# Output tiles of four tokens by 32 positions, and twelve of 28 weight pairs split into two words at each use

## The chip, the cores and the metric

One core of a Trainium2 chip runs the whole program. The metric is the device time of one execution in microseconds. Three runs of the kernel before gave 1483.95, 1479.09 and 1470.52 us, median 1479.09. TensorE multiplies (PE, its weight loads PEld), VectorE (DVE) and ScalarE (ACT) do elementwise work, GpSimd (POOL) and SyncE (SP) issue the DMAs.

## What is computed

Inputs are eight sequences of 576 positions; everything is in 32-bit floats.

```python
p_packed = attention(p, k, v)             # 32 packed queries a head, 8 heads of 64
x = attention(q, p_packed, p_packed)      # [8, 576, 512]
# mixer: xk, xr mix each position with the one before it
kk = relu(xk @ w_k) ** 2                  # 512 -> 1024
x = sigmoid(xr @ w_r) * (kk @ w_v)
# last block
u = x + (x.T @ U @ V).T                   # mixes positions, rank 32
out = u + relu(u @ w_ch1) @ w_ch2         # 512 -> 2048 -> 512
```

The first two parts take about the first half of the time, the last block the second.

## The kernel before

Each 32-bit operand of a matmul is split into a high part that a matmul takes exactly and a low rest ("hi" by a copy to the type fp32r, "lo" by a subtraction), and each product is three matmuls: hi by hi, hi by lo, lo by hi (`PASS`). The last block's two layers are each done with seven block products instead of eight (sums of blocks are formed first). Its weights are combined once, while the mixer runs (`make_ws`, `make_t`), split, and put in DRAM: 56 first-layer products lie in 28 pairs `ws_d0` to `ws_d27`, 512 KB each, and the second layer's in `t_d`.

The 36 token tiles of 128 tokens are worked on in six **steps** (s = 0 to 5) of six tiles. A step is a **window A** (`window_a`: first layer, 8 blocks f of 7 products, 336 matmuls named psc) and a **window B** (`window_b`: second layer, seven stages of 48 matmuls named psX, psY, psZ, psW). Weights come from DRAM again in every step, a pair at a time, through a ring of six tiles (`load_w`, pool `ring`, issued from POOL's queue; a load waits until PE is done with the pair six before). In A, ACT takes products out of PSUM (`p`, `hid`) and DVE sums them into `hid`; in B, ACT and DVE split `hid` into `sp` (three tiles) for PE.

Next to that, the step after is prepared. In A: SP loads its rows of x (`load_u`, tiles `u`, from `x2_d`, which the trace calls x_d) and, where a new pair of sequences begins, `xa` from `xu_d` (`load_xu`); DVE and ACT make `X` of xa (`sum_xu`); PE forms psh from X and the stretched V (`vst`); DVE adds it to u (`h_block`), turns it (`t_block`, 32 by 32 blocks), SP stores the turned tile to `uq_d` and loads it back in another order into `y` (`Turned.fill`). In B, ACT and DVE make the next step's operands `ob` from y (`operand_steps`). The results are added into y and turned back (`o`), and SP stores them (`send`).

A tile was 64 positions by two tokens i (`halves_of`: 576 positions of a sequence are 64 rows by 9 tokens; the ninth token has a tile of its own for both sequences). So a u load was two DMAs of 64 rows, and a tile's output eight stores of 32 KB: four by 128 columns, two by token.

The order on every engine is made before the run by the class `Plan`: each operation has predecessors, priority class and an assumed cost, and `emit` walks through time and gives every engine the operation it finds ready first; DVE and ACT take the earliest ready, PE and SP the earliest written. On the chip each engine takes its instructions strictly in this order, and so does each DMA queue's issuing engine.

Of the kernel before, what the change touches and what calls it, by code (L numbers as in the profile page):

```python
# [9 lines left out]
F32 = mybir.dt.float32  # L10
# [486 lines left out]
def packed_attention_moe_mixer_kernel(  # L497
# [707 lines left out]
    vst_ = []  # L1205

    def make_v():
        vst = plan.tile(vx_p, [P, 12, 64], F32R, "vst")
        vst_.append(vst)
        plan.zero(vst[:, NI:NI + 2].bitcast(F32))  # L1210
        for c in range(2):
            raw = plan.tile(st_p, [P, 512], F32, "s", parts=(0, 1, 2, 3), name="raw_v")
            for g in range(4):
                plan.dma(raw.at(g)[g * 32:(g + 1) * 32, 0:288], v_d[:, c * 288:(c + 1) * 288])
            rv = raw[:, 0:288].rearrange("p (c i) -> p i c", i=NI)
            to = vst[:, 0:NI, c * 32:(c + 1) * 32]
            plan.copy(to, rv, ("dve",))
            for g in (1, 3):
                gr = slice(g * 32, (g + 1) * 32)
                plan.tt(to[gr], rv[gr], to[gr], sub)  # L1220
        plan.copy(vst[:, NI + 2], vst[:, NI - 1], ("dve",))
# [33 lines left out]
    def make_ws(f):  # L1255
        a11, a12, a21, a22 = [t[:, h * 256:(h + 1) * 256] for t in raw_pair(w1_d, f) for h in range(2)]
        s1, s2, s3, s4 = four_sums()
        plan.tt(s1, a21, a22, add)
        plan.tt(s2, s1, a11, sub)
        plan.tt(s3, a11, a21, sub)  # L1260
        plan.tt(s4, a12, s2, sub)
        for i, src in enumerate((a11, s2, s1, a12, s3, s4, a22)):
            n, h = divmod(ws_at[f, i], 2)
            put_split(bl_ws, src, ws_d[n].at(h)[:, h * 512:(h + 1) * 512])

    def make_t(f):
# [12 lines left out]
        plan.tt(t3, b12, b22, sub)  # L1279
        plan.tt(t4, b21, t2, sub)  # L1280
        g, h = divmod(f, 2)
        for i, src in enumerate((b11, b21, b22, t4, t1, t2, t3)):
            put_split(bl_ws, src, t_d[i][g].at(h)[:, h * 512:(h + 1) * 512], by_block)

    def load_w(src):
        t = plan.tile(ring_p, [P, 2, 2, 256], F32R, "ring")
# [17 lines left out]
            plan.tt(X[64:128, :], xa[64:128], X[64:128, :], sub)  # L1304
            xt[b, b2] = X

    def halves_of(T):
        b, t = divmod(T, NI)
        if t == NI - 1:
            return b, [(slice(0, P), t, slice(0, P))]  # L1310
        b2, k2 = divmod(t, 4)
        return b, [(slice(e * 64, (e + 1) * 64), 2 * k2 + e, slice(b2 * 64, (b2 + 1) * 64)) for e in range(2)]

    def slot(n, name):
        if n < 4:
# [1 line left out]
        return plan.tile(st_p, [P, DM], F32, "s", parts=(0, 1), name=name)  # L1317

    def u_of(T):
        return ug[T][0]  # L1320

    def load_u(T, after=()):
        b, hs = halves_of(T)
        if T >= 6:
            u = slot(T % 6, "u")
            ug[T] = u, u.at(0), u.at(1)
        else:
            t = T % 2
            if t == 0:
                first_u[T] = plan.tile(cv.st, [P, 2, DM], F32, "st", parts=(0, 1, 2, 3), name="u")  # L1330
            u = first_u[T - t][:, t]
            ug[T] = u.on((2 * t, 2 * t + 1)), u.on(2 * t), u.on(2 * t + 1)
# [9 lines left out]
    def h_block(T, after=()):  # L1342
        b, t = divmod(T, NI)
        ps = plan.bank(prep_banks[0], "psh", prep_banks[0] is ps_a,
                       [plan.wr[x] for x in u_of(T).keys()] + list(after))
        if t < NI - 1:
            k2 = t % 4
            plan.mm(ps, vst_[0][:, 2 * k2:2 * k2 + 2].rearrange("p e c -> p (e c)"), xt[b, t // 4],
                    start=True, stop=True)
        else:  # L1350
            for b2 in range(2):
                plan.mm(ps, vst_[0][:, NI - 1 + 2 * b2:NI + 1 + 2 * b2].rearrange("p e c -> p (e c)"), xt[b, b2],
                        start=(b2 == 0), stop=(b2 == 1))
        u = u_of(T)
        if T >= 6:
            plan.tt(u, ps, u, add)
            return
        to = slot(T, "u") if T < 4 else first_u[0].on((2 * T - 8, 2 * T - 7))[:, T - 4]
        plan.tt(by_channel(to, "j m"), by_channel(ps, "m j"), by_channel(u, "m j"), add)
        ug[T] = (to,)  # L1360

    class Turned:

# [71 lines left out]
    def operand_steps(s):  # L1435
# [8 lines left out]
        for i, src in enumerate((b11, t2, t1, b21, t1, b22, t2)):  # L1444
# [27 lines left out]
    def product(s, f, i, ps, fresh):  # L1472
        n, e = divmod(ws_at[f, i], 2)
        if e == 0:
            wpair[0] = load_w(ws_d[n])
        w, x = wpair[0][:, e], ops[s][i]
        out = ps[:, 0:CW]
        c = 0
        for k in range(2):
            for wi, a in PASS:  # L1480
                plan.mm(out, w[:, wi, k * P:(k + 1) * P],
                        half(x, a)[:, k * CW:(k + 1) * CW],
                        start=(fresh and c == 0), stop=(c == 5), skip_group_check=True)
                c += 1
# [251 lines left out]
    for s in range(NS):  # L1736
        prep = {f: [] for f in range(NF)}
        more = iter(())
        if s + 1 < NS:
# [3 lines left out]
            for n in range(6):  # L1743
# [50 lines left out]
```

## Time and profile before

| | |
|---|---|
| runs, median (lowest to highest) | 1479.09 us (1470.52 to 1483.95) |
| the profiled execution | 1474.71 us, span 1472.9 us |
| PE busy / DVE / ACT / POOL | 95% / 75% / 48% / 18% of the span |
| mean granted TensorE clock | 0.972 |
| moved by DMA | 349.5 MB, 237 GB/s over the span |
| steps 0 to 5 begin at | 701, 829, 951, 1093, 1218, 1342 us; the last matmul ends near 1458 us |

The profile is of one execution. Times are from the start of its span. In rows of groups, "L259 DVE TENSOR_TENSOR sp<-hid,sp" is an instruction of VectorE that line 259 of the kernel (a helper) issued, writing a tile named sp and reading hid and sp. An idle time is put down to what ended it.

### The profile page before, as it was taken

How to read it: one execution, taken by the hardware profiler on the slowest of the kernel's cores; microseconds unless marked ns; L12 is line 12 of the kernel's file. 1: busy time of each engine (PE TensorE's matmuls, PEld its weight loads, DVE VectorE, ACT ScalarE, POOL GpSimd, SP SyncE). 2: the span in 40 equal slices, each digit the busy share in tenths (PEclk: the TensorE clock that was granted, in tenths of full speed). 3: DMA queues.
4: the chain of work that ended last, by engine and by line, in shares of the span. 5: the costliest groups of instructions: out<-in, count | busy, mean ns of one | idle time of the engine just before them, and what ended most of it. 6: DMA issues, size and time to landing. Idle time of an engine off the chain costs nothing.

```text
span 1472.9 us, 24029 instructions
## 1 busy us (share of the span) xinstructions
PE 1400.9 (95%) x8464; PEld 1277.0 (87%) x8464; DVE 1100.1 (75%) x2125; ACT 701.2 (48%) x1395; POOL 265.6 (18%) x502
## 2 busy tenths in 40 slices
PE   7889999999999999999998999979898999999996
PEld 5557888888888888888998998969798999999995
DVE  6777968778888989888577767836675795696475
ACT  5657656666666767676224223312332342242231
POOL 0000011321111111000222222212122222222220
PEclk8789999999999999999999999989999999999998
DMA  8853347767665768788998999999899989999985
GB/s 233 249 167 137 114 108 169 194 147 182 158 174 166 250 242 279 270 308 280 272 301 230 286 305 302 258 281 248 235 267 302 316 251 298 307 266 289 264 251 136
DMA packets 224584, 349.50 MB, mean 237 GB/s; under 512 B 92912, under 2 KB 138800, under 8 KB 224464
## 3 DMA queue, kind: packets, MB, share of 16 engines
q0 software_dynamic: 59264, 210.94, 48.4%
q1 hardware_dynamic: 165200, 137.02, 34.2%
q8 instruction: 67, 1.10, 0.3%
q14 instruction: 53, 0.43, 0.1%
HBM read 273.35 MB, written 74.52 MB: 236 GB/s over the span
## 4 chain that ended last, share of the span: by engine, by line
PE 65%; issue 14%; DMA 9%; POOL 4%; ACT 3%; DVE 3%; SPq 2%; POOLq 0%; DVEq 0%; ACTq 0%
PE psv L197 12%; PE psk L197 12%; PE psc L197 10%; PE psX L197 7%; PE psr L197 7%; PE psZ L197 4%; PE psat L197 4%; POOL ring L324 4%; PE psat L213 2%; PE psY L197 2%; PE psW L197 2%; DMA u<-x_d 2%; SPq L324 2%; DMA kin<-in_k_dram 1%; DMA ring<-t_d 1%
## 5 line engine op out<-in xcount | busy, mean ns | idle before, releaser
L197 PE MATMUL psc<-ob,ring 128*128 128x384 f32 x2016 | 358.8, 337 | 1.8 <-DVE hid L259 1.7
L197 PEld LDWEIGHTS psc<-ob,ring 128*128 128x128 f32 x2016 | 354.2, 190 | 5.1 <-DVE hid L259 2.7
L197 PE MATMUL psv<-w,kk 128*128 128x512 f32 x783 | 200.9, 395 | 0.0
L197 PE MATMUL psX<-sp,ring 128*128 128x384 f32 x864 | 161.5, 343 | 16.2 <-ACT sp L293 11.2
L259 DVE TENSOR_TENSOR hid<-p,psc 128x384 f32<-128x384 f32 x144 | 78.8, 549 | 130.4 <-PE psc L197 130.3
L293 ACT ACTIVATE p<-psc 128x384 f32<-128x384 f32 x96 | 47.3, 492 | 263.4 <-PE psc L197 255.8
L197 PEld LDWEIGHTS psX<-sp,ring 128*128 128x128 f32 x864 | 153.9, 193 | 21.3 <-ACT sp L293 12.5
L197 PEld LDWEIGHTS psv<-w,kk 128*128 128x128 f32 x783 | 144.5, 188 | 29.1 <-issue 2.3
L293 ACT ACTIVATE sp<-hid 128x768 fp32r<-128x768 f32 x120 | 100.7, 845 | 120.3 <-PE psX L197 56.2
L259 DVE TENSOR_TENSOR sp<-hid,sp 128x768 fp32r<-128x768 f32 x120 | 113.5, 952 | 48.4 <-ACT sp L293 47.6
L324 POOL DMA_DIRECT2D ring<-ws_d x168 | 90.4, 538 | 313.2 <-PE psc L197 233.7
L324 POOL DMA_DIRECT2D ring<-t_d x168 | 90.3, 538 | 286.5 <-PE psX L197 130.3
L197 PE MATMUL psk<-xk,w 128*128 128x384 f32 x528 | 104.4, 340 | 0.3 <-DVE w L278 0.3
L197 PE MATMUL psZ<-sp,ring 128*128 128x384 f32 x576 | 101.8, 334 | 0.0
L197 PEld LDWEIGHTS psZ<-sp,ring 128*128 128x128 f32 x576 | 100.0, 188 | 0.0
L197 PEld LDWEIGHTS psk<-xk,w 128*128 128x128 f32 x528 | 92.8, 188 | 5.4 <-DVE w L278 0.8
L197 PE MATMUL psr<-wA,xr 128*128 128x512 f32 x315 | 86.8, 403 | 0.0
L238 ACT ACTIVATE sq<-psk 128x384 f32<-128x384 f32 x96 | 46.4, 489 | 72.2 <-PE psk L197 71.6
L278 DVE SCALAR_TENSOR_TENSOR hid<-hid 128x384 f32<-128x384 f32 (+1 forms) x96 | 72.3, 753 | 3.1
L197 PEld LDWEIGHTS psr<-wA,xr 128*128 128x128 f32 x315 | 58.9, 192 | 13.1 <-issue 0.9
L324 POOL DMA_DIRECT2D st<-in_moe_w_ch_dram x80 | 44.0, 554 | 136.1 <-DVE m L278 128.9
L238 ACT ACTIVATE sp<-hid 128x768 fp32r<-128x768 f32 x48 | 40.7, 848 | 56.3 <-PE psX L197 41.0
(199 smaller groups left out, 2364.2 us busy)
## 6 DMA issues: line engine op xcount, KB each, us to landing
ring<-ws_d POOLq DMA_DIRECT2D x168, 512.0 KB, 5.1
ring<-t_d POOLq DMA_DIRECT2D x168, 512.0 KB, 4.8
ws_d<-bl SPq DMA_DIRECT2D x56, 256.0 KB, 4.1
t_d<-bl SPq DMA_DIRECT2D x56, 256.0 KB, 3.9
x_d<-xo SPq DMA_DIRECT2D x16, 576.0 KB, 3.3
x_d<-x POOLq DMA_DIRECT2D x36, 256.0 KB, 2.8
kin<-in_k_dram SPq DMA_DIRECT2D x32, 256.0 KB, 5.6
vin<-in_v_dram SPq DMA_DIRECT2D x32, 256.0 KB, 3.6
```

The source lines that it names most:

```text
L197: self.nc.tensor.matmul(o, l, r, start=start, stop=stop, **k)
L213: self.nc.tensor.transpose(out.get(), in_.get(), ident.get())
L238: self.nc.scalar.activation(o, in_.get(), func, **k)
L259: return self.elem(engs, lambda e, o, x, y: e.tensor_tensor(out=o, in0=x, in1=y, op=op), out, [a, b], self.TT, cls)
L278: ("dve",), lambda e, o, x, y: e.scalar_tensor_tensor(out=o, in0=x, scalar=s, in1=y, op0=op0, op1=op1), out, [a, b], self.TT, cls)
L293: self.nc.scalar.activation(o, i, AF.Copy)
L324: (self.nc.sync if eng == "sp" else self.nc.gpsimd).dma_start(out=o, in_=i)
```

## The change

Three things change. First, a tile is now 32 positions by four tokens (`rows_of`). A u load is one DMA, a tile's output four stores of 64 KB (24 stores in every step), and `vst` is laid out so that four tokens by 32 columns stand together. Second, of the 28 pairs the twelve with odd numbers from 5 to 27 (`RAW`) stay as plain 32-bit words in DRAM, 256 KB each. `make_ws` writes the block sums there without splitting them, and in every step `load_words` loads the words into one of four buffers, ACT copies hi into a ring tile and DVE subtracts for lo. Two of the buffers are spare parts of the operand tiles (`spare`), two lie in a tile that the mixer used (`words`). Third, t_block is listed for block 4 + n // 3 in place of 4 + n // 2.

```diff
+    RAW = tuple(range(5, 28, 2))
-    ws_d = [dtile(f"ws_d{n}", [P, 1024], (0, 1)) for n in range(7 * NF // 2)]
+    ws_d = [dtile(f"ws_d{n}", [P, (1024, 512)[n in RAW]], (0, 1)) for n in range(7 * NF // 2)]
...
             n, h = divmod(ws_at[f, i], 2)
-            put_split(bl_ws, src, ws_d[n].at(h)[:, h * 512:(h + 1) * 512])
+            if n in RAW:
+                plan.dma(ws_d[n].at(h)[:, h * 256:(h + 1) * 256], src)
+            else:
+                put_split(bl_ws, src, ws_d[n].at(h)[:, h * 512:(h + 1) * 512])
...
+    words = {}
+
+    def load_words(s, src):
+        if not words:
+            t = plan.tile(ust_p, [P, NI * P], F32, "ust", parts=(0, 1), name="words")
+            words.update((i, t.at(i)[:, i * 512:(i + 1) * 512]) for i in range(2))
+        i = words["n"] = words.get("n", -1) + 1
+        raw = words[i % 2] if i % 4 > 1 else spare[s, i % 2]
+        plan.dma(raw, src, eng="pool", slack=2000.0)
+        t = plan.tile(ring_p, [P, 2, 2, 256], F32R, "ring", parts=(0, 1))
+        hi, lo = [t.at(a)[:, :, a] for a in range(2)]
+        raw = raw.rearrange("p (e c) -> p e c", e=2)
+        plan.copy(hi, raw, ("act",))
+        plan.tt(lo, raw, hi, sub)
+        return t
...
-    def halves_of(T):
+    def rows_of(T):
         b, t = divmod(T, NI)
         if t == NI - 1:
-            return b, [(slice(0, P), t, slice(0, P))]
-        b2, k2 = divmod(t, 4)
-        return b, [(slice(e * 64, (e + 1) * 64), 2 * k2 + e, slice(b2 * 64, (b2 + 1) * 64)) for e in range(2)]
+            return b, slice(0, P), slice(t, NI)
+        w, i = divmod(t, 2)
+        return b, slice(w * 32, (w + 1) * 32), slice(4 * i, 4 * i + 4)
...
-        for n, (to, i, rows) in enumerate(hs):
-            dst = ug[T][1 + n] if len(hs) > 1 else ug[T][0]
-            plan.dma(dst[to], x2_d[b].at(i)[rows, i * DM:(i + 1) * DM], after=after)
+        src = x2_d[b].on(tuple(range(i.start, i.stop)))[rows, i.start * DM:i.stop * DM]
+        plan.dma(ug[T], src.rearrange("p (a c) -> a p c", c=DM) if i.stop - i.start > 1 else src, after=after)
...
-            wpair[0] = load_w(ws_d[n])
-        w, x = wpair[0][:, e], ops[s][i]
+            wpair[0] = load_words(s, ws_d[n]) if n in RAW else load_w(ws_d[n])
+        w = [wpair[0].on(a if n in RAW else 0)[:, e, a] for a in range(2)]
+        x = ops[s][i]
...
-                for to, i, rows in hs:
-                    plan.dma(dst[rows, i, m * P:(m + 1) * P].rearrange("(a p) c -> p a c", p=32),
-                             src[:, to.start // 32:to.stop // 32])
+                to = dst[:, :, m * P:(m + 1) * P]
+                if i.stop == NI:
+                    to = to.rearrange("(a p) i c -> p (a i) c", p=32)
+                plan.dma(to, src)
...
-                prep[4 + n // 2].append(lambda o, T=T: t_block(T))
+                prep[4 + n // 3].append(lambda o, T=T: t_block(T))
```

What moves shows in the orders. On SP, from the end of step 1 into window A of step 2 (x_d is `x2_d`, out_dram the output), there stood:

```order
L324 DMA y<-uq_d_234 32x4x384 x4
L324 DMA out_dram<-o 32x2x128 x40
L324 DMA out_dram<-o 32x4x128 x4
L324 DMA u<-x_d_71 64x512 x8
L324 DMA xa<-xu_d_75 32x512 x8
L324 DMA uq_d_235<-turned 128x1536
```

and now stands:

```order
L324 DMA y<-uq_d_234 32x4x384 x4
L324 DMA out_dram<-o 32x4x128 x24
L324 DMA u<-x_d_71 128x1x512 x4
L324 DMA xa<-xu_d_75 32x512 x8
L324 DMA uq_d_235<-turned 128x1536
```

Ahead of the xa loads SP has 24 stores and 4 loads in place of 44 and 8.

On ACT, at the end of window A and the first stages of window B of step 2 (p and hid are window A's last, the three ob copies make the next step's operands from y, sums are built from y too), there stood:

```order
L293 ACTIVATE p_11162<-psc_11223 128x384
L293 ACTIVATE ob<-y 128x4x6x32
L238 ACTIVATE hid<-psc_11201 128x384
L293 ACTIVATE ob<-y 128x4x6x32
L293 ACTIVATE sp<-hid 128x768
L238 ACTIVATE sp<-hid 128x768 x4
L293 ACTIVATE ob<-y 128x4x6x32
L293 ACTIVATE sp<-hid 128x768 x6
L293 ACTIVATE ob<-sums 128x4x6x32
```

and now stands:

```order
L293 ACTIVATE p_11135<-psc_11117 128x384
L238 ACTIVATE hid<-psc_11114 128x384
L293 ACTIVATE ob<-y 128x4x6x32 x2
L293 ACTIVATE sp<-hid 128x768
L238 ACTIVATE sp<-hid 128x768 x4
L293 ACTIVATE sp<-hid 128x768 x2
L293 ACTIVATE ob<-y 128x4x6x32
L293 ACTIVATE sp<-hid 128x768 x2
L293 ACTIVATE ob<-sums 128x4x6x32
```

The third ob copy stands behind seven sp copies in place of five; in step 0 it is seven in place of six.

On DVE, in the middle of window A of step 2, where X is made for the next step (u, turned: the next step's tiles; hid: this step's sums), there stood:

```order
L278 SCALAR_TENSOR_TENSOR hid<-hid 128x384
L296 CAST X_9986<-xa 128x512
L259 TENSOR_TENSOR hid<-p_10759,psc_10941 128x384
L259 TENSOR_TENSOR X_9981<-xa,X_9981 64x512
L259 TENSOR_TENSOR X_9986<-xa,X_9986 64x512
L259 TENSOR_TENSOR hid<-p_10854,psc_10993 128x384
L259 TENSOR_TENSOR u<-psh,u 128x512 x2
L220 STREAM_TRANSPOSE turned<-u 128x16x32 x2
L259 TENSOR_TENSOR hid<-p_10854,psc_10993 128x384
```

and now stands:

```order
L259 TENSOR_TENSOR ring<-words,ring 128x2x256
L278 SCALAR_TENSOR_TENSOR hid<-hid 128x384
L259 TENSOR_TENSOR hid<-p_10723,psc_10860 128x384
L259 TENSOR_TENSOR X_9932<-xa,X_9932 64x512
L259 TENSOR_TENSOR hid<-p_10801,psc_10920 128x384
L259 TENSOR_TENSOR X_9935<-xa,X_9935 64x512
L259 TENSOR_TENSOR u<-psh,u 128x512 x2
L220 STREAM_TRANSPOSE turned<-u 128x16x32
L259 TENSOR_TENSOR ring<-ob,ring 128x2x256
L259 TENSOR_TENSOR hid<-p_10801,psc_10920 128x384
L220 STREAM_TRANSPOSE turned<-u 128x16x32
```

The subtractions for lo (ring<-words, ring<-ob) stand between the hid sums, X at the same place among them; both casts of X are ACT's now.

## Rows read from the trace of the kernel before

**Rows 1.** Stages: us, busy PE PEld DVE ACT POOL (instructions), clock, DMA share, GB/s.

```profile
340.00:700.00 360.00, 359.11 (x2075) 308.33 (x2075) 315.32 (x713) 243.83 (x535) 48.09 (x91) 1.00 0.72 230
...
700.60:761.40 60.80, 60.80 (x350) 59.92 (x349) 36.37 (x66) 16.10 (x30) 16.15 (x30) 1.00 0.98 274
761.40:829.20 67.80, 61.66 (x338) 60.01 (x338) 52.48 (x68) 25.48 (x31) 15.06 (x28) 0.95 0.93 260
...
951.40:1026.00 74.60, 63.01 (x348) 62.33 (x348) 38.84 (x71) 16.33 (x30) 15.05 (x28) 0.91 0.98 263
1026.00:1093.40 67.40, 60.85 (x333) 59.84 (x333) 50.96 (x66) 24.73 (x30) 15.05 (x28) 0.95 0.91 244
1093.40:1160.20 66.80, 62.57 (x345) 61.57 (x344) 38.53 (x70) 16.45 (x30) 15.05 (x28) 0.95 1.08 304
1341.60:1399.80 58.20, 58.20 (x337) 58.20 (x336) 29.75 (x55) 14.36 (x27) 15.06 (x28) 1.00 0.97 287
1399.80:1458.20 58.40, 58.40 (x337) 58.09 (x336) 44.36 (x63) 21.21 (x25) 12.36 (x23) 1.00 0.80 228
```

**Rows 2.** PE's waits from 700 us on: total us, times, longest.

```profile
PE psh L197 <- DVE X L259: 15.7, 2, 11.6
PE psX L197 <- ACT sp L293: 11.2, 4, 5.7
PE psX L197 <- DMA ring<-t_d: 2.6, 4, 1.2
```

**Rows 3.** Waits of the whole run, same columns.

```profile
DVE hid L259 <- PE psc L197: 131.7, 113, 3.5
...
ACT ob L293 <- DMA y<-uq_d: 31.5, 9, 9.4
...
DVE X L296 <- DMA xa<-xu_d: 16.5, 2, 11.6
```

**Rows 4.** Timeline of SP's issues, 930 to 1010: start, us taken, count.

```profile
948.60 25.50 SPq L324 DMA_DIRECT2D out_dram<-o  x44
974.14 5.38 SPq L324 DMA_DIRECT2D u<-x_d  x8
979.57 9.28 SPq L324 DMA_DIRECT2D xa<-xu_d  x8
```

**Rows 5.** Timeline of PE in B0 and in B2; idle time before in brackets.

```profile
786.95 0.69 PE L197 MATMUL psX<-sp,ring 128*128 128x384 f32 x1 [4.64 <-ACT sp L293]
...
1048.59 0.69 PE L197 MATMUL psX<-sp,ring 128*128 128x384 f32 x1 [5.71 <-ACT sp L293]
```

**Rows 6.** DMA, 1024 to 1047: POOL's q0, SP's q1 (packets, MB); issues.

```profile
q0 software_dynamic: 1737, 6.33, 89.8%
q1 hardware_dynamic: 1467, 1.29, 41.7%
...
y<-uq_d SPq DMA_DIRECT2D x8, 96.0 KB, 14.1
```

**Rows 7.** DMA issues, 951 to 1012: count, KB, median us to landing.

```profile
y<-uq_d SPq DMA_DIRECT2D x3, 96.0 KB, 5.1
out_dram<-o SPq DMA_DIRECT2D x4, 64.0 KB, 4.8
```

**Rows 8.** Groups by line and form, 690 to 1473: busy us, mean ns.

```profile
L259 DVE TENSOR_TENSOR X<-xa,X 64x512 fp32r<-64x512 f32 x6 | 3.9, 688 | 0.1
L293 ACT ACTIVATE X<-xa 128x512 fp32r<-128x512 f32 x3 | 1.9, 631 | 12.2 <-DMA xa<-xu_d 12.0
```

**Rows 9.** SP's last stores: four of 64 KB, then 24 of 32 KB.

```profile
1455.94 1.83 SPq L324 DMA_DIRECT2D out_dram<-o  x4
...
1459.31 11.12 SPq L324 DMA_DIRECT2D out_dram<-o  x24
```

**Rows 10.** DMA issues, 1440 to 1473: columns as in rows 7.

```profile
out_dram<-o SPq DMA_DIRECT2D x40, 32.0 KB, 1.6
out_dram<-o SPq DMA_DIRECT2D x4, 64.0 KB, 1.8
```

More of the change, by code (lines that the diff above doesn't have):

```diff
@@ L1207, in make_v @@
     def make_v():
-        vst = plan.tile(vx_p, [P, 12, 64], F32R, "vst")
+        vst = plan.tile(vx_p, [P, 768], F32R, "vst")
         vst_.append(vst)
-        plan.zero(vst[:, NI:NI + 2].bitcast(F32))
+        plan.zero(vst[:, 576:704].bitcast(F32))
         for c in range(2):
@@ L1215, in make_v @@
             rv = raw[:, 0:288].rearrange("p (c i) -> p i c", i=NI)
[L1216 to L1221, printed above, removed]
+            for to, i0, i1 in ((vst[:, c * 256:(c + 1) * 256], 0, 8), (vst[:, 512 + c * 32:544 + c * 32], 8, NI)):
+                to = to.rearrange("p (i c) -> p i c", c=32)
+                plan.copy(to, rv[:, i0:i1], ("dve",))
+                for g in (1, 3):
+                    gr = slice(g * 32, (g + 1) * 32)
+                    plan.tt(to[gr], rv[gr, i0:i1], to[gr], sub)
+        plan.copy(vst[:, 704:768], vst[:, 512:576], ("dve",))
     def raw_pair(src, f):
@@ L1283, in make_t @@
             put_split(bl_ws, src, t_d[i][g].at(h)[:, h * 512:(h + 1) * 512], by_block)
+    words = {}
[12 more added lines that the diff above has]
+        return t
+    spare = {}
     def load_w(src):
@@ L1319, in u_of @@
     def u_of(T):
-        return ug[T][0]
+        return ug[T]
     def load_u(T, after=()):
-        b, hs = halves_of(T)
+        b, rows, i = rows_of(T)
         if T >= 6:
-            u = slot(T % 6, "u")
-            ug[T] = u, u.at(0), u.at(1)
+            ug[T] = slot(T % 6, "u")
         else:
@@ L1329, in load_u @@
             if t == 0:
-                first_u[T] = plan.tile(cv.st, [P, 2, DM], F32, "st", parts=(0, 1, 2, 3), name="u")
-            u = first_u[T - t][:, t]
-            ug[T] = u.on((2 * t, 2 * t + 1)), u.on(2 * t), u.on(2 * t + 1)
-        for n, (to, i, rows) in enumerate(hs):
-            dst = ug[T][1 + n] if len(hs) > 1 else ug[T][0]
-            plan.dma(dst[to], x2_d[b].at(i)[rows, i * DM:(i + 1) * DM], after=after)
+                first_u[T] = plan.tile(cv.st, [P, 2, DM], F32, "st", parts=(0, 1), name="u")
+            ug[T] = first_u[T - t].on(t)[:, t]
+        src = x2_d[b].on(tuple(range(i.start, i.stop)))[rows, i.start * DM:i.stop * DM]
+        plan.dma(ug[T], src.rearrange("p (a c) -> a p c", c=DM) if i.stop - i.start > 1 else src, after=after)
     prep_banks = [ps_a]
@@ L1346, in h_block @@
         if t < NI - 1:
-            k2 = t % 4
-            plan.mm(ps, vst_[0][:, 2 * k2:2 * k2 + 2].rearrange("p e c -> p (e c)"), xt[b, t // 4],
+            plan.mm(ps, vst_[0][:, t % 4 * P:(t % 4 + 1) * P], xt[b, t // 4],
                     start=True, stop=True)
@@ L1351, in h_block @@
             for b2 in range(2):
-                plan.mm(ps, vst_[0][:, NI - 1 + 2 * b2:NI + 1 + 2 * b2].rearrange("p e c -> p (e c)"), xt[b, b2],
+                plan.mm(ps, vst_[0][:, 512 + b2 * P:640 + b2 * P], xt[b, b2],
                         start=(b2 == 0), stop=(b2 == 1))
@@ L1357, in h_block @@
             return
-        to = slot(T, "u") if T < 4 else first_u[0].on((2 * T - 8, 2 * T - 7))[:, T - 4]
+        to = slot(T, "u") if T < 4 else first_u[0].on(T - 4)[:, T - 4]
         plan.tt(by_channel(to, "j m"), by_channel(ps, "m j"), by_channel(u, "m j"), add)
-        ug[T] = (to,)
+        ug[T] = to
     class Turned:
@@ L1452, in operand_steps @@
                 pl, tag = ((w1a, "wC"), (xin_p, "x"))[i - 2]
-                t = plan.tile(pl, [P, 2, 1024], F32R, tag, parts=(0, 1), name="ob")
-                t = tuple(t.at(a)[:, a, 0:768] for a in range(2))
+                t = plan.tile(pl, [P, 2048], F32R, tag, parts=(0, 1, 2), name="ob")
+                spare[s, i - 2] = t.at(2).bitcast(F32)[:, 1536:2048]
+                t = tuple(t.at(a)[:, a * 768:(a + 1) * 768] for a in range(2))
             else:
@@ L1480, in product @@
             for wi, a in PASS:
-                plan.mm(out, w[:, wi, k * P:(k + 1) * P],
+                plan.mm(out, w[wi][:, k * P:(k + 1) * P],
                         half(x, a)[:, k * CW:(k + 1) * CW],
@@ L1552, in send @@
         for t in range(3):
-            b, hs = halves_of(6 * s + 3 * h + t)
-            dst = out[2 * b:2 * b + 2].rearrange("b (p i) f -> (b p) i f", i=NI)
+            b, rows, i = rows_of(6 * s + 3 * h + t)
+            dst = out[2 * b:2 * b + 2].rearrange("b (p i) f -> (b p) i f", i=NI)[rows, i]
             o = slot(3 * n + t, "o")
```

## The prediction

> **What bounds the kernel now.** I read the stage times first, then what TensorE (PE) waits for in them, then the queue behind each wait. The last half is six steps, each a window A (336 first-layer matmuls) and a window B (336 second-layer ones). In [rows 1] one row is one stage: 340 to 700 us is the end of the mixer, then A0, B0, A2, B2, A3, A5 and B5. PE is busy in all of 340:700 (359.1 of 360.0 us), and A5 and B5 (58.2 and 58.4 us) are windows in which nothing disturbs it. A0, which also holds the small matmuls of the next step's preparation, takes 60.8. Against 60.8, A2 is 13.8 us long and A3 6.0; against 58.4, B0 is 9.4 and B2 9.0. These four excesses, 38.2 us, are what can be won there; they hold PE's idle time and the lower granted clock around it (0.91 and 0.95 against 1.00 in the same rows).
>
> [Rows 2] name the waits: PE waits 15.7 us for X on DVE, 11.2 us for sp on ACT, 2.6 us for a ring load. [Rows 3] show what stands behind: DVE's cast of X waits 16.5 us for the DMA of xa, and ACT's copy into ob waits 31.5 us for y. Both engines take their instructions in order, so hid, p and sp behind such a copy wait too, and with them PE. The third row of the group is the spare side: DVE idles 131.7 us in hid, waiting for PE.
>
> Why xa is late is in SP's queue in A2 [rows 4]: 44 stores take 25.50 us, 8 loads of u 5.38, and only at 979.57 do the 8 loads of xa begin. The longest wait for it is 11.6 us, in A2; the rest of PE's 15.7, 4.1 us, is A3's, where the queue has the same form.
>
> **The stores and xa.** A step of 48 stores (44 where it has the odd ninth tile) becomes 24, and u loads come one to a tile instead of two. What a 64 KB store costs on SP I bound by two rows: at the end of the run four 64 KB stores take 1.83 us and twenty-four of 32 KB 11.12 us [rows 9], 0.46 us each in either case, so a store costs by the piece of queue work and not by its bytes. In A2, beside ring loads, 32 KB stores take 0.58 each (25.50/44), and 64 KB ones land after a median 4.8 us [rows 7]. The other bound is that cost follows bytes, 1.16 us for 64 KB; I take 0.58. Then A2's queue is 24 x 0.58 = 13.9 us of stores and 4 x 0.67 = 2.7 of u, and xa begins 16.6 us after 948.60, at 965.2: 14.4 us earlier. The wait was 11.6 us, so it is gone, with 2.8 us to spare. In A3 (4.1 of the 15.7 us) the margin is larger. Behind X comes the first psh, which the order leaves in its place. Of 13.8 + 6.0 = 19.8 us I take **19**.
>
> **The tail.** After the last matmul SP issues 24 stores, from 1459.31 on for 11.12 us [rows 9]; now they are 12. That is 12 x 0.46 = 5.6 us less, and the last one lands 0.2 us later (1.8 against 1.6) [rows 10]: **5.4** us, on the path by itself. By bytes it would be 0.
>
> **The y loads and ACT.** B0 and B2 stall because ACT's third copy of a step (ob from y, second half) waits for y while later sp copies stand behind it; PE idles 4.64 and 5.71 us there [rows 5]. The order of the changed kernel puts this copy behind 7 sp copies where it stood behind 6 (step 0) and 5 (step 2). One sp feeds 12 matmuls, 2.08 us by the undisturbed pace (58.2/336 x 12). So the stalls shrink by 2.08 and 4.16 us, **6.2** in all, if y comes when it comes now; bounds are 0 (y later by as much) and 18.4 (both excesses).
>
> Does y come earlier, since the loads of window A shrink? 72 ring loads move 256 KB less (18.9 MB). But the second y loads run in the first part of B, where ring loads stay what they are. There y lands after 14.1 us, with 1737 packets of POOL's queue against 1467 of SP's in the stretch [rows 6]; where the X wait had emptied the queue, y landed in 5.1 [rows 7]. So what counts is whether ring loads run beside it, and I leave y where it is. If landing went by bytes instead, 3.1 MB less of 14.7 in a window A (21%) would take 14.1 to 11.1 us, and the 2.6 and 1.6 us that remain would go too: 4 us more.
>
> The Trainium skill, "DMA: Bandwidth & Descriptors", section "Queues, rings and completion order", says that each DMA engine takes turns between the queues that have work, a packet at a time. That speaks against a gain from smaller ring loads: SP's small packets get their turn just the same as long as POOL's queue has any work. By it the sum below stands; by bytes it would be 4 us lower. The near equal packet counts agree with it.
>
> **The splits at use.** 12 of 28 pairs are loaded as words and split by ACT (hi) and DVE (lo) into the ring: 72 copies at 0.631 us and 72 subtractions at 0.688 [rows 8], 45 us of ACT and 49.5 of DVE. ACT is busy 16.1 of 60.8 us in A0, so its 7.6 per window lie beside PE. DVE is busy 36.4 of 60.8 there and gets 8.3 more. The split of pair n needs the ring slot of pair n-6 and is needed five pairs later, 10.4 us; the words are loaded further ahead, into four buffers of their own. Critical is only the middle of a prepared A, where h, turn and X also stand in DVE's order, with four subtractions. Bounds: 0, since DVE idles 131.7 us on PE [rows 3], and 5 windows x 4 x 0.688 = 13.8 us if none of these find a gap. I take **2**, near the lower end, as A0 has 24 idle us. POOL keeps the same number of ring issues; a words load waits for the subtraction four words earlier and holds the ring load behind it, but that subtraction stands early enough in DVE's order (pair 5's just after B's last sums).
>
> Earlier, 24 half splits with their stores of 256 KB fall away in 340:700 (now 128 KB as they are): PE has 0.9 us of idle time there, so **0**. The other layout of vst, the turn-blocks listed one hidden pair earlier and the u loads' shape cost nothing: turn still comes at the same place among the hid instructions, since DVE takes what is ready first.
>
> **Sum.** 1474.7 (this execution; span 1472.9) - 19 - 5.4 - 6.2 + 2 = **1446**. The median of the runs shown, 1479.1, is 4.4 above this execution; I leave the forecast on the execution's scale, since the waits that go hang on when a DMA lands, which may well be what differs between those runs.
>
> **Rivals.**
> *y comes early* (20%): for it, window A has room on the DMA engines; against it [rows 6]. Then B0's and B2's 18.4 us go whole: 1474.7 - 19.8 - 18.4 - 5.4 = 1431; with the 2.6 us of ring waits 1428.
> *DVE lags in the prepared windows, or part of the X wait stays* (15%): 1474.7 - 19 - 5.4 + 13.8 = 1464 without help from ACT's order, down to 1454 with it and half the lag.
> *Stores cost by bytes* (6%): SP is 24 x 1.16 = 27.8 us in stores, xa begins no earlier (2.3 us later in each of A2 and A3), the tail stays: 1474.7 + 4.6 - 6.2 + 2 = 1475. [Rows 9] speak against it.
> *Slower: the subtractions are on the path* (4%). In every A the chain load, ACT, DVE, PE would be late by the subtraction itself: 72 x 0.688 = 49.5 us, 1474.7 - 19 - 5.4 + 49.5 = 1500. It decides once DVE has no idle time ahead of a split, that is once its 24 us of idle in an A are down to under 8; the rows say three times as much.
> *The change does little of what it says* (5%): the first copy or cast in the new order meets another late DMA (u, say), and the waits move: about 1470.
>
> **Chances and range.** My forecast has 50% (1437 to 1454). Under 1%, 14.8 us, a change can't be told from none here. Faster by more (under 1464.3): forecast, early y and lag, 85%. Within 1%: bytes and moved waits, 11%. Slower: 4%. The range of 8 in 10 runs from all of both terms, 1428, to the lag with no help, 1463.
>
> **What would show it.** In the changed profile A2 and A3 should be within 2 us of A0, DVE should not wait for xa, and SP should spend about 14 us on 24 stores. The tail after the last matmul should be near 10 us instead of 15. B0 and B2 should be near 63, with ACT still waiting for y; at 59 y came early. Subtractions into ring should show no wait of PE on DVE over 1 us. PE waiting for ring from DVE, or A windows all 5 us longer, would make the prediction wrong, as would X waiting still.

## The result, and the profile after

The changed kernel takes 1486.85 us (median of 11 runs, 1482.86 to 1492.88) against 1475.77 us (11 runs, 1469.69 to 1483.95): a ratio of 1.0077, 95% interval 1.0052 to 1.0103. It is slower by 0.8%, where 1446 us was forecast. Below, one profiled execution of it: 1486.33 us, span 1484.1.

Its stages A0, B0, A2, B2, A3, B3 and B5, columns as in [rows 1]:

```profile
700.70:770.40 69.70, 63.46 (x354) 60.99 (x353) 44.45 (x80) 23.65 (x43) 18.49 (x34) 0.95 0.73 218
770.40:839.40 69.00, 62.27 (x338) 61.40 (x337) 52.57 (x68) 24.70 (x30) 15.05 (x28) 0.95 0.97 253
...
965.20:1037.50 72.30, 61.82 (x344) 60.85 (x343) 44.50 (x81) 22.53 (x41) 15.21 (x28) 0.93 0.78 213
1037.50:1113.00 75.50, 62.53 (x337) 60.88 (x337) 52.59 (x68) 26.39 (x32) 15.05 (x28) 0.93 0.88 236
1113.00:1173.20 60.20, 60.20 (x346) 59.67 (x345) 45.27 (x82) 23.40 (x42) 15.20 (x28) 1.00 0.90 262
1173.20:1237.80 64.60, 60.60 (x338) 59.67 (x337) 53.32 (x74) 24.77 (x30) 15.06 (x28) 0.97 1.00 266
...
1416.20:1474.60 58.40, 58.40 (x338) 58.12 (x336) 44.37 (x63) 21.22 (x25) 12.37 (x23) 1.00 0.80 229
```

Against [rows 1], A0 is 8.9 us longer, B2 8.1, while A3 is 6.6 shorter; A2, of which 13.8 us were to go, is still 72.3. From the last matmul to the end of the span it is 1484.1 - 1474.6 = 9.5 us, where it was 14.7.

PE's waits from 690 us on (total, times, longest), which answer to [rows 2]:

```profile
PE psY L197 <- DMA ring<-t_d: 12.9, 4, 3.5
PE psX L197 <- ACT sp L293: 11.1, 2, 8.4
PE psh L197 <- DVE X L259: 10.5, 1, 10.5
PE psu L197 <- DVE x L259: 6.2, 1, 6.2
```

The waits for X and sp are still there, with two new ones: t_d ring loads, 2.6 to 3.5 us in each of B0 to B3, and x at the start of A0. Behind X and sp stand xa and y as before [rows 3].

SP's queue in A2, which answers to [rows 4]:

```profile
961.75 14.80 SPq L324 DMA_DIRECT2D out_dram<-o  x24
977.37 3.41 SPq L324 DMA_DIRECT2D u<-x_d  x4
980.83 25.89 SPq L324 DMA_DIRECT2D xa<-xu_d  x8
```

The 24 stores take 14.8 us, four u loads 3.4, as forecast (13.9 and 2.7). But the eight xa issues, 9.28 us in [rows 4], now take 25.89: SP stands still between them. The last is issued at 1006.7, and X is late again. What SP waits for are u loads under way: the first row is the changed kernel's, the second the kernel before's, from 690 and 700 us on (total, times, longest):

```profile
SPq L324 <- DMA u<-x_d: 63.6, 14, 9.9
...
SPq L324 <- DMA u<-x_d: 16.4, 15, 2.0
```

What runs meanwhile, in one microsecond (columns as in [rows 1]):

```profile
1005.00:1006.00 1.00, 0.00 (x0) 0.00 (x0) 0.00 (x0) 0.00 (x0) 0.00 (x0) 0.50 0.27 98
```

Every compute engine idles, xa is wanted, and yet the 16 DMA engines are busy for 0.27 of the time: about four of them work. All packets of this microsecond are of SP's queue.

Stalls of PE in B0 (two rows) and in B2 (idle time in brackets), which answer to [rows 5]:

```profile
782.35 10.18 PE L197 MATMUL psY<-sp,ring 128*128 128x384 f32 x48 [3.48 <-DMA ring<-t_d]
...
799.39 0.44 PE L197 MATMUL psX<-sp,ring 128*128 128x384 f32 x1 [2.70 <-ACT sp L293]
...
1073.50 0.69 PE L197 MATMUL psX<-sp,ring 128*128 128x384 f32 x1 [8.44 <-ACT sp L293]
```

The stall for sp in B2 has grown from 5.71 to 8.44 us; in B0 it is 2.70 instead of 4.64, after 3.48 us lost to a t_d load.

### The profile page after: what moved, and what is told of

Same layout as the page of the kernel before. It is cut to its first block, busy times and chain, and to the rows that moved or that the text cites. A ratio compares the mean times of both kernels' runs of the same rounds, so it can differ in the third digit from the quotient of the medians.

```text
span 1484.1 us, 24008 instructions
## 1 busy us (share of the span) xinstructions
PE 1403.1 (95%) x8464; PEld 1277.2 (86%) x8464; DVE 1136.2 (77%) x2181; ACT 737.1 (50%) x1441; POOL 267.0 (18%) x502
## 4 chain that ended last, share of the span: by engine, by line
PE 65%; DMA 18%; DVE 5%; issue 5%; ACT 4%; SPq 1%; POOL 1%; DVEq 0%; POOLq 0%; ACTq 0%
PE psc L197 13%; PE psv L197 10%; PE psk L197 9%; PE psX L197 7%; PE psZ L197 7%; PE psr L197 6%; DMA u<-x_d 6%; PE psat L197 4%; PE psW L197 3%; DMA y<-uq_d 3%; PE psat L213 2%; DMA t_d<-bl 2%; PE psY L197 2%; DMA ring<-t_d 1%; DMA ring<-ws_d 1%
## 5 line engine op out<-in xcount | busy, mean ns | idle before, releaser
L197 PE MATMUL psX<-sp,ring 128*128 128x384 f32 x864 | 159.2, 340 | 15.5 <-ACT sp L293 11.1
L324 POOL DMA_DIRECT2D ring<-ws_d x96 | 51.9, 540 | 176.1 <-PE psc L197 113.2
L197 PE MATMUL psY<-sp,ring 128*128 128x384 f32 x288 | 56.4, 357 | 13.7 <-DMA ring<-t_d 12.9
```

The lines of the kernel that those rows point to most:

```text
L197: self.nc.tensor.matmul(o, l, r, start=start, stop=stop, **k)
L324: (self.nc.sync if eng == "sp" else self.nc.gpsimd).dma_start(out=o, in_=i)
```

## The experiments

**Theory U**: the u load as one DMA of 4 x 32 rows is what is slow; it uses few DMA engines and holds up what follows it. **Theory W**, my first rival: the word loads. POOL issues the next step's first four (1 MB) among t_d loads at the turn from A to B, and the first splits at A0's start wait for ring slots. Those two come first below, by taking the parts of the change apart.

The table gives all runs. A and B are the sums of windows 0 to 4 in the profiled execution (A5 and B5 are 116.6 or 116.7 us together in all of them); the border between an A and the next B is uncertain by some 2 us, since their matmuls mix. A0's start differs by some 4 us between executions even where nothing ahead of it was changed (700.6 in the kernel before, 696.8 in later_copy), so smaller differences there say nothing.

| kernel | median us | ratio to before, 95% | A0 starts | A | B | tail |
|---|---|---|---|---|---|---|
| before | 1472.6 to 1477.6 | 1 | 700.6 | 321.2 | 319.8 | 14.7 |
| the change | 1486.9 | 1.0077 [1.0052, 1.0103] | 700.7 | 322.2 | 335.1 | 9.5 |
| u_in_four | 1434.2 | 0.9714 [0.9682, 0.9746] | 698.1 | 299.0 | 307.1 | 9.5 |
| no_words | 1511.6 | 1.0248 [1.0205, 1.0291] | 701.0 | 337.4 | 343.3 | 9.5 |
| words_alone | 1450.8 | 0.9822 [0.9778, 0.9866] | 701.8 | 306.7 | 314.2 | 14.7 |
| tiles_four_no_words | 1467.3 | 0.9924 [0.9887, 0.9960] | 698.6 | 313.7 | 321.8 | 9.6 |
| half_loads | 1454.0 | 0.9869 [0.9834, 0.9905] | 695.3 | 310.4 | 315.4 | 14.7 |
| words_and_bytes | 1479.4 | 1.0043 [1.0012, 1.0074] | 723.5 | 311.8 | 307.9 | 14.7 |
| before_one_u | 1617.9 | 1.0988 [1.0951, 1.1024] | 725.5 | 386.7 | 372.6 | 14.7 |
| u_in_four_16 | 1436.0 | 0.9758 [0.9733, 0.9784] | 696.8 | 300.1 | 312.9 | 9.5 |
| copies_in_step | 1453.0 | 0.9866 [0.9832, 0.9901] | 699.0 | 312.2 | 310.5 | 14.7 |
| u_whole | 1431.8 | 0.9734 [0.9701, 0.9768] | 697.2 | 299.3 | 306.8 | 9.5 |
| later_copy | 1456.2 | 0.9886 [0.9842, 0.9930] | 696.8 | 321.9 | 301.3 | 14.7 |
| whole_later_copy | 1427.5 | 0.9690 [0.9660, 0.9720] | 699.8 | 299.2 | 299.9 | 9.5 |

### u_in_four

```diff
-        plan.dma(ug[T], src.rearrange("p (a c) -> a p c", c=DM) if i.stop - i.start > 1 else src, after=after)
...
+        for a in range(4):
+            dst = ug[T].on(...)[a * 32:(a + 1) * 32]
+            plan.dma(dst, x2_d[b].at(i.start + a)[rows, (i.start + a) * DM:(i.start + a + 1) * DM], after=after)
```

> The changed kernel with each u load of 4 x 32 rows issued as four loads of 32 rows; words and stores as they are. Theory U (the one load of 4 x 32 x 512 lands slowly, and later loads of SP that reuse its semaphore wait for it): in A2 SP's eight xa issues take under 11 us in place of 25.9, PE's wait for X (10.5 us) is gone, in B2 the ACT sp wait of 8.4 us shrinks below 4, and the total falls by 18 to 26 us to 1461 to 1469; the waits for a t_d ring load in the B windows (12.9 us) stay, since they are put down to the word loads. If SP's queue at the start of A0 was held by the same loads, A0's 8.9 us go too: 1453 to 1460. Rival S (xa and y are late since 64 KB stores and the ring loads take the DMA engines): the 18 more loads a step cost SP some 0.6 us each, nothing else moves, 1484 to 1492.

The same bytes to the same place in four pieces: 53 us less than the change, more than theory U said. (Left out of the edit: the ninth token's tile, which stays one load, and the tiles' finer parts. The order on ACT and DVE is all but the same as in the change, by the two traces.) Its stages A0, B0, A2 and B2:

```profile
698.10:759.70 61.60, 61.60 (x353) 60.07 (x352) 43.20 (x79) 23.02 (x42) 17.17 (x32) 1.00 0.76 227
759.70:821.00 61.30, 59.31 (x339) 58.12 (x338) 52.14 (x68) 24.77 (x30) 15.06 (x28) 1.00 0.98 282
...
940.60:1000.30 59.70, 59.70 (x344) 59.43 (x344) 44.17 (x81) 24.01 (x43) 15.21 (x28) 1.00 0.95 266
1000.30:1063.50 63.20, 59.49 (x338) 58.08 (x337) 52.37 (x68) 24.65 (x30) 15.05 (x28) 1.00 1.01 275
```

PE's waits from 690 us on:

```profile
PE psY L197 <- DMA ring<-t_d: 5.2, 3, 2.1
PE psX L197 <- DVE sp L259: 2.0, 6, 0.6
PE psX L197 <- ACT sp L293: 1.2, 1, 1.2
```

And SP's queue in A2:

```profile
937.10 14.70 SPq L324 DMA_DIRECT2D out_dram<-o  x24
951.85 10.52 SPq L324 DMA_DIRECT2D u<-x_d  x16
962.41 6.14 SPq L324 DMA_DIRECT2D xa<-xu_d  x8
```

SP issues 16 u loads for four, 10.5 us instead of 3.4, and the last xa is still issued 31.5 us after the first store, where it was 45.0: the eight issues take 6.14 us. X no longer makes PE wait, A2 is 59.7. A0's start and most of the waits for t_d, which I had put down to the words, go as well. At A0's start the cause was the same: from 684 to 702 us SP waits 7.8 us for u loads in the changed kernel. Its queue there:

```profile
686.48 12.22 SPq L324 DMA_DIRECT2D xa<-xu_d  x8
698.75 1.39 SPq L324 DMA_DIRECT2D t_d<-bl  x3
```

The eight xa issues took 12.22 us, and three t_d stores stood behind them. These stores read what lies in ring slots that the first splits write. ACT's split in the changed kernel:

```profile
705.68 0.63 ACT L293 ACTIVATE ring<-ob 128x512 fp32r<-128x512 f32 x1 [9.84 <-DMA t_d<-bl]
```

DVE's half of it stood ahead of x, and PE waited 6.2 us for x. In u_in_four the xa issues are over by 691 us and PE has no such wait. Rival S falls, and with it most of W.

### no_words, words_alone, tiles_four_no_words

```diff
-    RAW = tuple(range(5, 28, 2))
+    RAW = ()
```

> The changed kernel with all 28 weight pairs split beforehand as in the kernel before (no words, no splits at use); tiles, u loads and stores as changed. Theory W (word loads of the next step stand among the t_d ring loads at the turn from A to B, and cost some 3.4 us in each of B0 to B3; the first splits at A0's start wait for slots and hold x back, 8.9 us): ring waits of PE in B under 4 us in all in place of 12.9, A0 back at 60 to 62 us, A2 and B2 still long (72 and 73 to 76) by the u loads; total 1460 to 1468. If A0's start belongs to the u loads alone, A0 stays near 69 and the total is 1469 to 1476. Rival (the word loads help, since they move fewer bytes, and the ring waits come from elsewhere): the ring waits stay, total 1484 to 1495.

> The kernel before with the words alone: 12 of 28 pairs kept as words and split at use, while tiles, u loads (two of 64 rows) and the 48 stores a step stay. Theory W: ring waits of PE in B rise from 2.6 to 10 to 16 us, X waits as before (15.7), so 1484 to 1490; with the start of A0 held as in the changed kernel (if splits alone do that) up to 1497. Rival as in the prediction (the splits lie beside other work, plus 2): 1474 to 1480 and ring waits under 5 us.

> The changed kernel with u loads in fours of 32 rows and without words: the new tiles and stores alone. Theories U and W together: no X wait, no B ring wait, A0 near 61, A2 61 to 66, B2 60 to 66; the tail 10 us; total 1442 to 1452 (the prediction's sum without the splits, 1444, and up to 8 us if the 12 more u issues on SP in A2 bring part of the X wait back). If U is wrong, A2 and B2 stay long and it is 1462 or more; if W is wrong, 1455 or more with ring waits over 8 us.

The edit above made no_words from the change, and tiles_four_no_words from u_in_four; words_alone is the kernel before with `RAW`, `load_words`, `spare` and their use in `product` and `make_ws` added. Theory W is wrong: without the words the change is 25 us slower, and words alone make the kernel before 27 us faster. So both my theory and the prediction had the sign of the words wrong, and the times of no_words and words_alone lie in none of the ranges that I had given for them. tiles_four_no_words is 15 us above its 1442 to 1452: A2 and B2 stay at 69.8 and 71.1 us. Its 16 u issues take 11.30 us in A2, so that xa begins 27.5 us after the first store, where it was 31.0; the prediction had 16.6. Two by two, from these four and the kernel before (1477.6 beside them):

- words: 1477.6 to 1450.8 with the old tiles, 1467.3 to 1434.2 with the new ones: -27 and -33 us;
- tiles with u in fours: -10 us without words, -17 with them, of which the tail is 5.2;
- the u load in one piece: 1467.3 to 1511.6 without words, 1434.2 to 1486.9 with them: +44 and +53 us.

### before_one_u

```diff
-        for n, (to, i, rows) in enumerate(hs):
-            dst = ug[T][1 + n] if len(hs) > 1 else ug[T][0]
-            plan.dma(dst[to], x2_d[b].at(i)[rows, i * DM:(i + 1) * DM], after=after)
+        i, rows, n = hs[0][1], hs[0][2], len(hs)
+        src = x2_d[b].on(tuple(range(i, i + n)))[rows, i * DM:(i + n) * DM]
+        plan.dma(ug[T][0], src.rearrange("p (a c) -> a p c", c=DM) if n > 1 else src, after=after)
```

> The kernel before with the two u loads of a tile (64 rows each) issued as one of 2 x 64 x 512; everything else as before. Theory U (such a load uses only as many DMA engines as its first dimension allows: four in the changed kernel, and only two here): the transfer of 256 KB takes about twice as long as there, xa and y behind it late, 1510 to 1580. Rival M (the loads in the changed kernel were late since the words, the stores or four rows of x apart made them so): half the issues, 1470 to 1480.

Half the u issues, and 145 us slower, beyond the range of theory U; 25 us of it lie ahead of A0. Stretches of 2 us in the longest wait for X, and the matmul that ends it:

```profile
1078.00:1080.00 2.00, 0.00 (x0) 0.00 (x0) 0.00 (x0) 0.00 (x0) 0.00 (x0) 0.50 0.13 48
1080.00:1082.00 2.00, 0.00 (x0) 0.00 (x0) 0.00 (x0) 0.00 (x0) 0.00 (x0) 0.50 0.13 48
...
1085.06 1.22 PE L197 MATMUL psh<-X,vst 128*128 128x512 f32 x2 [25.95 <-DVE X L259]
```

0.13 of 16 DMA engines is two, where the change showed about four (0.27). Two is the first dimension of 2 x 64 x 512, four that of 4 x 32 x 512. Half the first dimension gives half the share: theory U is shown, with its dose. Rival M, 1470 to 1480, is far off.

### half_loads

```diff
+    def load_half(src):
+        t = plan.tile(ring_p, [P, 2, 2, 256], F32R, "ring")
+        plan.dma(t[:, 0].rearrange("p a c -> p (a c)"), src.at(0)[:, 0:512], eng="pool")
+        return t
...
-            wpair[0] = load_w(ws_d[n])
-        w, x = wpair[0][:, e], ops[s][i]
+            wpair[0] = (load_half if n in HALF else load_w)(ws_d[n])
+        w, x = wpair[0][:, 0 if n in HALF else e], ops[s][i]
```

> The kernel before, where the ring load of the same 12 pairs moves only its first half (256 KB of 512 KB) and the pair's second product uses the first one's weights, so that the second product's result is not the reference's; no splits at use, tiles, stores and u loads as before. Theory B (the 27 us that words alone gave come from the 3.1 MB less that each window A's ring loads move): 1440 to 1452, xa's eight issues in A2 near 5.7 us, ACT's wait for y near 20 us or less in place of 31.5. Rival O (they come from the other order, ACT and DVE taking the splits and X's casts): 1470 to 1480, xa's issues 9 us.

Fewer bytes without splits gave 19 us: a little below theory B's gain, far from rival O. But it was not bytes alone. `Plan` reckons a load's cost from its bytes, so the order was made anew too: in B2 the third ob copy stands behind six sp copies, where it stood behind five, and DVE's order differs in many places. ACT still waits 27.2 us for y, and not the 20 of theory B. Its waits:

```profile
PE psh L197 <- DVE X L259: 8.5, 1, 8.5
PE psX L197 <- ACT sp L293: 4.8, 2, 3.5
PE psY L197 <- ACT sp L238: 3.7, 1, 3.7
```

The gain is mostly in the A windows (-10.8 us, with X's wait down from 15.7 to 8.5); xa lands 6.7 us after its issue in A2, where it was 8.2. 5.3 us are A0's earlier start, of which later_copy, with nothing changed ahead of A0, has 3.8 too. B0, whose order on ACT is that of before, stays at 67.3; B2 is 7.7 us shorter.

### words_and_bytes, copies_in_step

```diff
-        plan.dma(raw, src, eng="pool", slack=2000.0)
+        op = plan.dma(raw, src, eng="pool", slack=2000.0)
+        plan.dma(pad, src, after=[op], eng="pool")
```

> The kernel before with words alone, as in words_alone, and with each word load a copy of the same 256 KB from DRAM to DRAM behind it on POOL's queue, so that a window A moves the bytes it moved before. Theory B: the gain goes, 1470 to 1500 (the copies also write to memory, so somewhat slower than before is possible). Rival O: it stays, 1448 to 1456.

In this one the copies had nothing to wait for and were issued early, most before A0, which starts 22 us later than in words_alone for it; in the steps next to nothing changed (A and B together 619.7 us, 620.9 in words_alone). It tells nothing of theory B. The second has the edit above:

> As words_and_bytes, whose copies all ran early, before the first window A, and so tested nothing in the steps; here each copy of 256 KB from DRAM to DRAM is issued on POOL's queue only after its word load of the same step. Theory B (bytes beside SP's loads decide): the gain of words alone goes, 1466 to 1495, with xa's eight issues in A2 at 8 to 10 us instead of 5.7 and DMA shares in the A windows back to 0.97 and more. Rival O (the order of ACT and DVE gave it): 1448 to 1457.

The first three rows are its waits, the last is words_alone's:

```profile
PE psh L197 <- DVE X L259: 11.8, 2, 9.5
PE psY L197 <- DMA ring<-t_d: 8.1, 7, 2.4
PE psX L197 <- DMA ring<-t_d: 1.7, 2, 1.1
...
PE psh L197 <- DVE X L259: 4.8, 1, 4.8
```

In time rival O has it: 1453. In the profile each is half right: the bytes bring the wait for X back (4.8 in words_alone, 11.8 here), the xa issues take 7.83 us in place of 5.65, and the A windows grow by 5.5 us; but PE's waits for sp on ACT do not come back. Here too `Plan` made another order, so bytes and order are not taken apart; what it speaks for is that the bytes alone are not the 27 us of words_alone.

### later_copy

```diff
-            plan.copy(hi, src, ("act",) if s else ("act", "dve"))
+            op = plan.copy(hi, src, ("act",) if s else ("act", "dve"))
+            if s and i == 5:
+                op.preds[sp_op[11]] = 1
```

(`sp_op` lists a window B's sp copies in order; the twelfth is its third stage's last.)

> The kernel before with one edit: ACT's third ob copy of a step (from y's second half) stands behind ten sp copies in place of five to seven; tiles, loads, stores and DVE's order as before. Theory A (the order on ACT, and not bytes, is what shortens the B windows in words_alone and in copies_in_step): PE's 11.2 us of waiting for sp on ACT fall below 4, B0 and B2 come to 60 to 63 us, A2 stays at 72 to 75 with its wait for X; 1462 to 1470, ratio 0.990 to 0.997. Rival D (DVE's sums from y wait for the same load and take the stall over): B0 and B2 stay above 65, ratio 0.998 to 1.003.

```profile
PE psh L197 <- DVE X L259: 15.2, 2, 12.4
PE psX L197 <- DMA ring<-t_d: 4.9, 5, 1.4
PE psZ L197 <- ACT sp L293: 1.6, 1, 1.6
```

Its B0 and B2, columns as in [rows 1]:

```profile
757.60:821.50 63.90, 60.84 (x338) 59.57 (x338) 52.59 (x68) 26.46 (x32) 15.05 (x28) 0.97 1.01 281
...
1017.00:1077.20 60.20, 60.13 (x343) 59.26 (x344) 51.93 (x69) 24.87 (x30) 15.05 (x28) 1.00 1.05 280
```

One copy put behind a few others on ACT: 1.1% faster, with B windows 18.5 us shorter, A windows and the wait for X as they were. By the traces the order on DVE, SP and POOL is the same as before, so this run changes ACT's order alone. Theory A holds, and gives more than it said. The same copy shows in the others. In the kernel before it waited 8.37 us for y in B0. In half_loads, behind six sp copies as before, it waits nearly as long (ACT's timeline):

```profile
779.29 0.84 ACT L293 ACTIVATE ob<-y 128x768 fp32r<-128x768 f32 x1 [7.60 <-DMA y<-uq_d]
```

In words_alone, behind seven, it waits half of that:

```profile
785.03 0.85 ACT L293 ACTIVATE ob<-y 128x768 fp32r<-128x768 f32 x1 [3.56 <-DMA y<-uq_d]
```

### u_in_four_16, u_whole, whole_later_copy

> The changed kernel with u loads in fours and 16 of 28 pairs as words (12, 16, 20 and 24 too): window A moves 1 MB less again and splits 4 times more. Theory B, with what is left: A windows are 58.2 to 61.6 us with the DMA engines at 0.93 to 0.95 there and at 0.97 to 1.01 in B, so what remains is mostly in B, whose loads do not change: 1426 to 1434. Rival (DVE and ACT are late with more splits): 1436 to 1450, with PE waits for ring on DVE or ACT.

With `RAW` 16 pairs in place of 12 nothing is won (1436.0 against 1434.2): A stays, B is 5.8 us longer. PE waits 4.2 us for sp on DVE, where it waited 2.0, and 4.6 for sp on ACT (1.2): the rival of late splits, at its lower end.

```diff
+        for w in range(4):
+            r = (2 * w + i // 4) * P + i % 4 * 32 if i < NI - 1 else i * P + w * 32
+            plan.dma(x2_d[b].at(4 * i + w)[r:r + 32], x2[w * 32:(w + 1) * 32], eng="pool")
...
+        plan.dma(ug[T], x2_d[b].on(tuple(part))[t * P:(t + 1) * P], after=after)
...
```

> The changed kernel, words and all, with x2_d kept in the order of the tiles: a u load is one load of 128 x 512 from 256 KB in a row, and the mixer's 32 stores a pair of sequences go out in fours of 32 rows. Theory U: as fast as u loads in fours or faster, since SP issues 6 loads in place of 24 a step and the second y of B2 no longer stands behind 8 u loads (8.2 us): 1426 to 1436. Rival (one load of 256 KB is slow in itself, however it is cut): 1475 to 1490. If the stores in fours hold POOL's queue in the mixer, the windows start later than 698 us.

One load of 128 x 512 is as fast as fours of 32 rows (the intervals overlap), though SP spends 2.58 us on u in A2 and not 10.52:

```profile
950.41 2.58 SPq L324 DMA_DIRECT2D u<-x_d  x4
953.04 7.19 SPq L324 DMA_DIRECT2D xa<-xu_d  x8
```

So it is not the size of the load that hurts, and SP's issues no longer decide. With later_copy's edit on top:

> u_whole with the edit of later_copy: the third ob copy behind nine or ten sp copies. What is left in u_whole of PE's waits is 1.8 us for sp on ACT, 3.9 for t_d ring loads and 1.8 for sp on DVE, so there is little to win: 1424 to 1431 if the sp wait and the part of B0 and B2 above 60 go with it; if y's second load is met in time already, no difference that can be told (1428 to 1435).

1427.5 us, 3.1% under the kernel before, the fastest of all. PE's waits from 690 us on that are left:

```profile
PE psY L197 <- DMA ring<-t_d: 4.7, 4, 1.7
PE psc L197 <- DMA ring<-ws_d: 0.2, 1, 0.2
```

## Why the prediction was wrong, step by step

**"The u loads' shape cost nothing": the step that failed.** It cost 44 to 53 us, four times what separates the change from the kernel before, and it turned the forecast's sign. I had counted a u load by its issues (four for eight) and its bytes, as I did for the stores, whose pieces of 32 rows by four tokens (32x4x128) are taken well. The u load puts the four ahead of the 32. The order shows it as `u<-x_d_71 128x1x512` where `64x512` stood; none of the rows that I had shows a load with a small first dimension, so it needed bounds from both sides, as the stores had them, and I gave it none. With DMA shares of 0.27 and 0.13 above, the runs show that a first dimension of four or two leaves about four or two of the 16 DMA engines with work.

The Trainium skill has a rule for this in "DMA: Bandwidth & Descriptors", section "Why a DMA increments its semaphore by 16 and not by 1": a DMA is spread over the largest number of engines up to 16 that divides the slowest dimension of both its sides. By it the change's load uses four engines, before_one_u's two, and 64, 32 or 128 rows all use 16; the traces agree (0.27, 0.13, and in u_whole u loads of the same 256 KB land after 6.9 us in A2 and PE has no wait for X).

Slow u loads reach PE in two ways. SP, issuing xa or y behind them, waits for them between its issues (63.6 us in all, 25.89 for eight xa). And ring loads, on POOL's queue, land later. In B0 POOL issues the load that psY begins with 1.62 us ahead of the first psX in the change and in u_in_four alike, but PE can start on it 13.6 and 11.5 us after its issue; and in every pair PE waits longer for ring loads beside the narrow u load, 16.4 us against 5.2 with words, 15.5 against 6.9 without, 6.2 in before_one_u against 3.1. That the few engines with u work have less time left for their share of the ring loads would explain it, but no run shows that, and none separates what either way costs.

Nor would the sum have come out without this step: u_whole, the change with a quick u load, takes 1431.8 us and not 1446, since the words' term had the wrong sign (below).

**The stores and xa (-19).** The arithmetic of the queue held: 14.8 us for 24 stores, and in u_whole xa begins 17.4 us after the first store, 16.6 by the forecast. In u_in_four and in u_whole A2 and A3 are 20.1 us shorter than before (72.9 + 66.8 to 59.7 + 59.9, by the table's borders), with words. In tiles_four_no_words they are 8.5 us shorter, and PE still waits 6.5 us for X; but there u takes 16 issues, and no run has quick u loads in four issues without words, so what the stores alone are worth stays open. What I had left out is that beside full ring loads the xa loads land later, 8.2 us after issue in the kernel before, and u loads 7.3. In words_alone, DMA issues of A2, columns as in [rows 7]:

```profile
u<-x_d SPq DMA_DIRECT2D x8, 128.0 KB, 5.9
...
xa<-xu_d SPq DMA_DIRECT2D x8, 64.0 KB, 6.3
```

**The tail (-5.4)**: 14.7 to 9.5, -5.2. Right, and with it that a store costs by the piece and not by bytes.

**ACT's order (-6.2)**: the mechanism is right, the size was not measured by itself. In words_alone, which has this order and the old u loads, B0 and B2 are 8.2 us shorter, but so are they in half_loads, where the copy moved by one place in B2 and by none in B0. In the changed kernel y was late instead (its second eight issues in B2 took 16.75 us behind the u loads, 6.09 in the kernel before). Moved further, as in later_copy, the copy alone was worth 18.5 us in the B windows. That this is near the 18.4 that I had named for B0 and B2 is chance: B0 and B2 give 12.8 of it (67.8 + 69.1 to 63.9 + 60.2, by the table's borders), B1 and B4 the rest. PE's 11.2 us of waiting go down to 1.6, and so does most of the low clock around them (0.95 in B0 and B2 [rows 1], 0.97 and 1.00 in later_copy).

**The splits (+2)**: as work they are hidden, as forecast. DVE's busy time in A0 goes from 36.4 to 43.2 us, A0 from 60.8 to 61.6 in words_alone, and no row shows PE waiting for a ring tile on ACT or DVE; what a split held up was x at A0's start, 6.2 us, when a late t_d store held up the split. But the sign was wrong: the words give 27 to 33 us. Their smaller ring loads, which I put at nothing, are likely part of it: half_loads gained 19 us with them and a somewhat other order. DMA shares of 0.98 and 1.08 in A2 and A3 [rows 1] could have made me ask how xa lands beside smaller loads, though a share near 1 doesn't say by itself that a load is late: A0 and A5 have 0.98 and 0.97 and lose nothing. I read instead y in B [rows 6], where ring loads do not change. There little moved, as forecast: in B2 y landed after 13.6 us in words_alone, 12.7 in half_loads, 14.1 before, and in B0 after 14.6 in half_loads, 12.0 before.

The rule that I weighed, that each DMA engine takes turns between queues by packets (the Trainium skill, "DMA: Bandwidth & Descriptors", "Queues, rings and completion order"), does not conflict with y, whose time changed little and in both directions. What I drew from it, that SP's loads gain nothing from smaller ring loads, was wrong for xa, which landed after 6.3 and 6.7 us in words_alone and half_loads instead of 8.2.

**"POOL keeps the same number of ring issues"**: true, and the four word loads at the turn seemed at first to cost 13 us. With u in fours the waits for t_d are 5.2 us, and in later_copy, which has no words, 4.9. So the words cost little there.

**The rivals.** Only the moved waits (5%) named a late u load, at 1470 and as an aside. None had a slower side by the load's shape. That y lands early, at 1428 to 1431, gives a time close to u_in_four's 1434, but not by that mechanism: y lands 12.2 us after its issue in its B2, 14.1 before, and ACT meets it later, behind seven sp copies. The lower end of the rival of lag, 1454, is also summed wrongly: 1464 less 6.2 and half of 13.8 is 1451. It changes no chance.

What stays open: how much of words_alone's 27 us is bytes and how much is order. Order alone gave 17 us (a larger move than the words make); smaller loads gave 19, with an order that moved too; both touch the same wait for y, and copies_in_step, which gives the bytes back as copies that nobody waits for, lost only 0.4% with intervals that overlap.

## What to carry to other kernels

When a DMA's access pattern is rewritten, look at its first dimension before its bytes and its count: a pattern that puts a four ahead of 32 rows kept about four of 16 DMA engines busy here, and what stood behind it in the queue paid, and so did the other queue's loads. When stages show DMA shares near 1, a byte less is worth pricing even if no wait names it. Where an in-order engine has one late copy in its list, with independent work behind it, moving that copy back was the cheapest gain here. And an edit that changes a load's size can change the order that a planner makes: compare the orders before calling a run a test of bytes alone.

## What the runs showed of the hardware

- A load of 2 x 64 x 512 keeps 0.13 of the 16 DMA engines busy and moves 48 GB/s when nothing else runs; one of 4 x 32 x 512 0.27 and 98 GB/s: about 24 GB/s an engine. With the same 256 KB as 128 x 512 or as four loads of 32 x 512, PE's wait for X is gone (10.5 us in the change).
- Taking 3.1 MB of 14.7 off the ring loads of a window A went with a faster landing of SP's loads beside them (xa 8.2 to 6.3 us, u 7.3 to 5.9), while y beside unchanged ring loads stayed at 13.6 us of 14.1 in B2.
- One copy on ACT that waited 8.37 us for its load, with work behind it, cost PE 4.64 us of idle time in B0 [rows 5]; moving it back in every step made the B windows 18.5 us shorter together, the lower clock around such stalls included.
